# A causal decay attention with its MLP on one core: decays of k put ahead of loads in one group, the opening written out by hand, the decay of the state on ScalarE

## The chip, the core and the metric

The kernel runs on one NeuronCore of a Trainium2 chip. The metric is the device time of one execution in microseconds, the median of several executions. The engines are TensorE (PE, its weight loads are PEld), VectorE (DVE), ScalarE (ACT), GpSimd (POOL) and SyncE (SP). Each works through its own instructions in the order in which the program gives them, and they wait for each other by semaphores. Loads that turn f32 into bf16 are issued by GpSimd; stores and DMA transposes are issued by SyncE.

## What is computed

A linear attention with a decay `lam` per head, over 4 batches, 8 heads, 768 positions and head size 64, and behind it an MLP with an exact GELU (512 to 2048 to 512) on the 3072 tokens:

```python
intra = einsum(qb, kb) * Dmask            # inside a block, lam ** (i - j) for i >= j
out   = intra @ vb + (qb * lam_pow) @ kv_state
kv_state = lam_block * kv_state + (kb * rev_pow).T @ vb
...
h = x @ w_in
g = 0.5 * h * (1.0 + erf(h / sqrt(2)))
y = g @ w_out
```

The kernel takes blocks of 128 positions instead of 64, which gives the same sums.

## The kernel before

**Tiling.** There are 24 chunks of 128 positions (`NCH`), 6 for each batch (`NB`). A chunk holds all 8 heads. Four chunks (`M`) make a group of 512 tokens, and there are 6 groups (`NG`). The MLP works by groups: `mlp_blocks` (L226) gives 16 first products `mm1` (L235, four matmuls of 512 columns into `h_ps`, then GELU on ScalarE, L237) and then the second products `mm2` (L247), four to a block, with a copy by ScalarE (L252) and a store by SyncE (L253) for each 128 tokens. The attention of group g + 1 is placed between the MLP blocks of group g; the attention of group 0 stands ahead of all of it and is called the opening here.

**A chunk's steps.** `begin` takes the loaded tiles q, k and v. `decay_k` (L146) makes `k_dec`, k times a decay: eight ScalarE instructions (L153) for chunks 0 and 1, else one GpSimd instruction (L155). `transposes` (L157) turns k and q by TensorE (L161) into one PSUM bank `t_ps`, and copies them out as `kT` and as `qT` (times the decay, L168). From chunk 8 on `dma_transposes` (L170) does it instead: SyncE issues a DMA transpose of k (L174), GpSimd makes `q_hat` (L175), and SyncE issues a DMA transpose of `q_hat` (L176). `scores` (L178) makes the scores `sc_ps` (L183), the state product `kv_ps` (L190), the masked scores `sc_m` on VectorE (L195), the new state `state` (L199, L201) and its decayed copy `old` (L204) that the next chunk's state adds: VectorE makes `old` in the opening, GpSimd later. `outputs` (L207) adds the product with the state (L213) and the one with `sc_m` (L217) in `o_ps` and casts it into the group's `x_t` (ScalarE L221 in the opening, VectorE L223 later). The last chunk of a batch (5, 11, 17, 23) needs no `k_dec` and no new state.

**What sets the order.** The order is written out by hand (`manual_schedule`). In the opening a loop over s (L299 to L311) issues `transposes` and `decay_k` of chunk s, `scores` of chunk s - 1 and `outputs` of chunk s - 2. GpSimd issues the 12 loads of chunks 0 to 3 first, then the weights, then the loads of chunks 4 to 7. For the later chunks the list `todo` (L319 to L326) gives each of four steps a due point on a scale of MLP cost: kind 0 (`begin`, the DMA transposes, `decay_k`, and `prefetch`, which issues the loads of the chunks up to n + 5), kind 1 (`transposes`, group 0's MLP only), kind 2 (`scores`), kind 3 (`outputs`). `first`, `end` and `fs` set these points; a step is issued before the first MLP block that reaches its point.

**Buffers.** q, k and v have 8 buffers each, the work tiles (`kT`, `qT`, `k_dec`, `state`, `old`, `sc_m`, `q_hat`) 3 each, and PSUM has one bank each for the tags `t` and `o` and two each for `sc`, `mh` and `mo`.

Of the kernel before, what the change touches and what calls it, by code (L numbers as in the profile page):

```python
# [15 lines left out]
def kernel(  # L16
# [23 lines left out]
    M = 4  # L40
# [8 lines left out]
    work_pool = ctx.enter_context(tc.tile_pool(name="work", bufs=3))  # L49
# [21 lines left out]
    pos = consts.tile([128, 1], F32)  # L71
# [21 lines left out]
    ident = consts.tile([128, 128], BF16)  # L93
# [3 lines left out]
    warm = consts.tile([128, 1], F32)  # L97
# [8 lines left out]
    lam_q = consts.tile([128, HP, C], F32)  # L106
# [3 lines left out]
    lam_c = consts.tile([128, HP], F32)  # L110
# [12 lines left out]
    lam_c_b = lam_c[:, :, None].to_broadcast((128, HP, D))  # L123

    def make_dmask():
        nc.vector.tensor_mul(dmask, cmask[:, None, :].to_broadcast((128, H, C)),
                             lam_m[:, :, None].to_broadcast((128, H, C)))
# [5 lines left out]
    xT = {}  # L133
    states = {}

    def bank(shape, dtype, tag, name):
        return ps.tile(shape, dtype, tag=tag, name=name, bufs=2 if tag in ("sc", "mh", "mo") else 1)

    def begin(n, early=False):
        c = Chunk()  # L140
        c.n, c.sb, c.early = n, n % NB, early
        c.sc_tag = "mo" if early and n % 2 else "sc"
        c.q, c.k, c.v = (raw.pop((n, name)) for name in "qkv")
        return c

    def decay_k(c, eng):  # L146

        if c.sb == NB - 1:
            return
        c.k_dec = work_pool.tile([128, H, D], BF16, tag="kd", name="k_dec")  # L150
        if eng is nc.scalar:
            for h in range(H):
                nc.scalar.activation(c.k_dec[:, h, :], c.k[:, h, :], ACT.Copy, scale=lam_k[:, h:h + 1])  # L153
        else:
            eng.tensor_mul(c.k_dec, c.k, lam_k[:, :, None].to_broadcast((128, H, D)))  # L155

    def transposes(c):  # L157
        t_ps = bank([128, 2, HP, C], BF16, "mh" if c.early else "t", "t_ps")
        for i, src in ((0, c.k), (1, c.q)):
            for hp in range(HP):  # L160
                nc.tensor.transpose(t_ps[:, i, hp, :], src[:, 2 * hp:2 * hp + 2, :], ident)  # L161
        c.kT = work_pool.tile([128, HP, C], BF16, tag="kT", name="kT")
        c.qT = work_pool.tile([128, HP, C], BF16, tag="qT", name="qT")
        if c.early:
            nc.scalar.copy(c.kT, t_ps[:, 0])
        else:
            nc.vector.tensor_copy(c.kT, t_ps[:, 0])  # L167
        nc.vector.tensor_mul(c.qT, t_ps[:, 1], lam_q)  # L168

    def dma_transposes(c):  # L170
        c.kT = work_pool.tile([128, HP, C], BF16, tag="kT", name="kT")
        c.qT = work_pool.tile([128, HP, C], BF16, tag="qT", name="qT")
        q_hat = work_pool.tile([128, H, D], BF16, tag="qh", name="q_hat")
        nc.sync.dma_start_transpose(out=c.kT, in_=c.k.rearrange("p h d -> p (h d)"))  # L174
        nc.gpsimd.tensor_mul(q_hat, c.q, lam_p[:, :, None].to_broadcast((128, H, D)))  # L175
        nc.sync.dma_start_transpose(out=c.qT, in_=q_hat.rearrange("p h d -> p (h d)"))  # L176

    def scores(c):  # L178
        sc_ps = [bank([128, HP, C], F32, c.sc_tag, f"sc_ps{hi}") for hi in range(2)]
        for hp in range(HP):  # L180
            for hi in range(2):
                p = slice(hi * D, (hi + 1) * D)
                nc.tensor.matmul(sc_ps[hi][:, hp, :], c.kT[p, hp, :], c.qT[p, hp, :], start=True, stop=True)  # L183
        more = c.sb < NB - 1
        if more:
            kv_ps = bank([128, HP, D], F32, "t", "kv_ps")
            for hp in range(HP):
                for hi in range(2):
                    h = 2 * hp + hi
                    nc.tensor.matmul(kv_ps[hi * D:(hi + 1) * D, hp, :], c.k_dec[:, h, :], c.v[:, h, :],  # L190
                                     start=True, stop=True)
        c.sc_m = work_pool.tile([128, HP, 2, C], BF16, tag="sc_m", name="sc_m")
        dmask_r = dmask.rearrange("p (hp hi) i -> p hp hi i", hi=2)
        for hi in range(2):
            nc.vector.tensor_mul(c.sc_m[:, :, hi, :], sc_ps[hi], dmask_r[:, :, hi, :])  # L195
        if more:
            new = work_pool.tile([128, HP, D], BF16, tag="state", name="state")
            if c.sb == 0:
                nc.vector.tensor_copy(new, kv_ps)  # L199
            else:  # L200
                nc.vector.tensor_add(new, kv_ps, states[c.n][1])  # L201
            old = work_pool.tile([128, HP, D], F32, tag="old", name="old")
            if c.sb < NB - 2:
                (nc.vector if c.early else nc.gpsimd).tensor_mul(old, new, lam_c_b)  # L204
            states[c.n + 1] = new, old

    def outputs(c, x_t, off):  # L207
        o_ps = bank([128, HP, C], F32, "o", "o_ps")
        if c.sb > 0:
            for hp in range(HP):  # L210
                for hi in range(2):
                    p = slice(hi * D, (hi + 1) * D)
                    nc.tensor.matmul(o_ps[p, hp, :], states[c.n][0][p, hp, :], c.qT[p, hp, :],  # L213
                                     start=(hp == 0), stop=False, skip_group_check=True)
        for hp in range(HP):
            for hi in range(2):
                nc.tensor.matmul(o_ps[hi * D:(hi + 1) * D, hp, :], c.v[:, 2 * hp + hi, :], c.sc_m[:, hp, hi, :],  # L217
                                 start=(c.sb == 0 and hp == 0), stop=True, skip_group_check=True)
        x_o = x_t[:, :, off * C:(off + 1) * C]
        if c.early:  # L220
            nc.scalar.copy(x_o, o_ps)  # L221
        else:
            nc.vector.tensor_copy(x_o, o_ps)  # L223
# [65 lines left out]
    def prefetch(upto):  # L289
        while next_load[0] <= min(upto, NCH - 1):  # L290
            for name in "kqv":
                load(next_load[0], name)
            next_load[0] += 1
# [2 lines left out]
    alloc_x(0)  # L296
    live = {}
    make_dmask()
    for s in range(M + 2):  # L299
        if s < M:  # L300
            live[s] = begin(s, early=True)
            if s == 2:
                load_w_in(0)
            transposes(live[s])
            decay_k(live[s], nc.scalar if s < 2 else nc.gpsimd)
            if s == 1:
                nc.scalar.activation(warm, pos, ACT.Gelu)
        if 0 <= s - 1 < M:
            scores(live[s - 1])
        if s >= 2:  # L310
            outputs(live[s - 2], xT[0], s - 2)  # L311
    for s in range(1, NS):
        load_w_in(s)
    for s in range(NS):
# [5 lines left out]
    for n in range(M, NCH):  # L320
        g, i = n // M - 1, n % M
        first, end = (0.66, 1.0) if g == 0 else (0.0, 0.97)
        at = lambda f: (g + first + (end - first) * (i + f) / M) * total
        fs = (-0.5, 0.0, 0.5, 1.05) if g == 0 else (-1.0, 0.0, 0.35, 0.75)
        todo += [(at(f), kind, n) for kind, f in enumerate(fs)]
    todo.sort()  # L326

    def step(kind, n):
        g = n // M - 1
        if kind == 0:  # L330
            live[n] = begin(n)
            if g > 0:
                dma_transposes(live[n])
            decay_k(live[n], nc.gpsimd)
            prefetch(n + 5)
        elif kind == 1:
            if g == 0:
                transposes(live[n])
        elif kind == 2:
            scores(live[n])  # L340
        else:
            outputs(live[n], xT[g + 1], n % M)

# [2 lines left out]
    for g in range(NG):  # L346
        if g + 1 < NG:
            alloc_x(g + 1)
        for run, cost in mlp_blocks(g):
            while todo and todo[0][0] <= done:  # L350
                step(*todo.pop(0)[1:])
            run()
            done += cost
        for item in [t for t in todo if t[2] // M == g + 1]:
            todo.remove(item)
            step(*item[1:])
# [30 lines left out]
```

## Time and profile before

| | us |
|---|---|
| median of 3 runs (lowest, highest) | 239.39 (237.59, 240.59) |
| the profiled execution, its own time | 239.67 |
| its span, first to last instruction | 237.5 |
| TensorE matmuls busy in it | 209.7 (88%) |
| GpSimd busy in it | 111.6 (47%) |
| ScalarE busy in it | 86.0 (36%) |
| VectorE busy in it | 62.7 (26%) |

The profile is one execution of the program. Busy time says how long an engine had an instruction under way; what sets the end is read from the places where TensorE waits. The chain that ended last gives 70% of the span to TensorE, 14% to GpSimd and 11% to DMA. The timeline lists instructions in order of time, merged where like follows like; a wait stands in brackets at the end, with what ended it. The windows view gives each engine's busy time, the granted clock of TensorE (1.00 is 2.4 GHz, 0.50 is 1.2 GHz) and the DMA share in stretches of the span.

### The profile page before, as it was taken

The numbers are of one execution on the slowest core, as the hardware profiler recorded it, in microseconds if no ns is written. First come the engines' busy times: TensorE is split into PE (matmuls) and PEld (weight loads), VectorE is DVE, ScalarE is ACT, GpSimd is POOL, SyncE is SP. The second block draws the span as 40 slices with busy tenths as digits, with TensorE's granted clock in tenths as the row PEclk, the third lists the DMA queues.
The fourth block names the chain that finished last, engine by engine and source line by source line (L and its number), as shares of the span: only waits on it lengthen the run. The fifth ranks groups of instructions, "written<-read, shape, count | busy, mean of one in ns | idle before, by whom it ended". The sixth has DMA issues, their size and how long they took to land.

```text
span 237.5 us, 3783 instructions
## 1 busy us (share of the span) xinstructions
PE 209.7 (88%) x1528; PEld 102.5 (43%) x1552; DVE 62.7 (26%) x111; ACT 86.0 (36%) x158; POOL 111.6 (47%) x132
## 2 busy tenths in 40 slices
PE   1576999993198999999999999999999999999994
PEld 0355344441044444444444444444444444444453
DVE  3396000264034333132223213222321323100000
ACT  6862365000004552106650125621056510266211
POOL 8997236899717949901684696004403200000000
PEclk9999999999569999999999999999999999999998
DMA  7999999999985999994969999601433101110012
GB/s 51 146 149 199 202 207 159 153 188 138 149 35 135 114 88 95 134 171 110 92 56 101 109 168 170 63 0 47 134 89 68 22 26 65 44 44 0 32 59 88
DMA packets 100272, 24.36 MB, mean 103 GB/s; under 512 B 92960, under 2 KB 97312, under 8 KB 100256
## 3 DMA queue, kind: packets, MB, share of 16 engines
q0 software_dynamic: 79104, 13.64, 79.7%
q1 hardware_dynamic: 21152, 10.50, 20.2%
q8 instruction: 12, 0.20, 0.4%
q14 instruction: 4, 0.03, 0.1%
HBM read 27.27 MB, written 6.29 MB: 141 GB/s over the span
## 4 chain that ended last, share of the span: by engine, by line
PE 70%; POOL 14%; DMA 11%; issue 3%; DVE 0%; ACT 0%; POOLq 0%
PE o_ps L247 30%; PE h_ps L235 30%; DMA w_out_t<-in_moe_w_out_dram 8%; DMA k_t<-in_k_dram 3%; POOL v_t L65 3%; POOL q_t L65 3%; POOL k_t L65 3%; PE o_ps L217 3%; PE sc_ps L183 2%; PE o_ps L213 2%; POOL k_dec L155 2%; PE kv_ps L190 2%; PE o_ps L262 1%; POOL w_in_t L87 1%; POOL w_out_t L91 1%
## 5 line engine op out<-in xcount | busy, mean ns | idle before, releaser
L235 PE MATMUL h_ps<-x_t,w_in_t 128*128 128x512 bf16 x372 | 88.0, 386 | 2.3 <-DVE x_t L223 0.8
L247 PE MATMUL o_ps<-w_out_t,g_t 128*128 128x512 bf16 x356 | 83.7, 385 | 1.8 <-issue 1.7
L237 ACT ACTIVATE g_t<-h_ps 128x512 bf16<-128x512 f32 x96 | 57.3, 597 | 41.0 <-PE h_ps L235 41.0
L235 PEld LDWEIGHTS <-w_in_t 128*128 128x128 bf16 x384 | 36.8, 99 | 45.5 <-issue 4.6
L247 PEld LDWEIGHTS <-g_t 128*128 128x128 bf16 x368 | 34.4, 99 | 40.4 <-issue 1.7
L252 ACT COPY o_sb<-o_ps 128x512 f32<-128x512 f32 x23 | 13.5, 585 | 96.0 <-PE o_ps L247 87.8
L195 DVE TENSOR_TENSOR sc_m<-sc_ps,dmask 128x512 bf16<-128x512 f32 x48 | 30.9, 685 | 62.5 <-PE sc_ps L183 62.5
L204 POOL TENSOR_TENSOR old<-state,lam_c 128x256 f32<-128x256 bf16 x12 | 7.3, 611 | 61.4 <-DVE state L201 35.3
L65 POOL DMA_DIRECT2D q_t<-in_q_dram x24 | 21.4, 894 | 5.4 <-DMA w_out_t<-in_moe_w_out_dram 3.3
L65 POOL DMA_DIRECT2D k_t<-in_k_dram x24 | 22.0, 915 | 3.7 <-DMA w_out_t<-in_moe_w_out_dram 1.7
L65 POOL DMA_DIRECT2D v_t<-in_v_dram x24 | 21.3, 889 | 5.0 <-DMA w_in_t<-in_moe_w_in_dram 1.7
L223 DVE CAST x_t<-o_ps 128x512 bf16<-128x512 f32 x20 | 13.8, 690 | 35.6 <-PE o_ps L217 35.6
L155 POOL TENSOR_TENSOR k_dec<-k_t,lam_k 128x512 bf16<-128x512 bf16 x18 | 19.0, 1058 | 0.0
L175 POOL TENSOR_TENSOR q_hat<-q_t,lam_p 128x512 bf16<-128x512 bf16 x16 | 16.7, 1046 | 0.0
L190 PE MATMUL kv_ps<-v_t,k_dec 128*64 128x64 bf16 x160 | 6.9, 212 | 10.5 <-POOL k_dec L155 9.1
L217 PE MATMUL o_ps<-sc_m,v_t 128*64 128x128 bf16 x192 | 10.8, 240 | 0.0
L183 PE MATMUL sc_ps<-qT,kT 64*128 64x128 bf16 x192 | 10.4, 233 | 0.3 <-DVE qT L168 0.2
L190 PEld LDWEIGHTS <-k_dec 128*64 128x64 bf16 x160 | 4.8, 119 | 12.9 <-POOL k_dec L155 9.3
L161 PE MATMUL t_ps<-ident,k_t 128*128 128x128 bf16 x32 | 4.2, 275 | 6.8 <-DMA k_t<-in_k_dram 6.3
L183 PEld LDWEIGHTS <-kT 64*128 64x128 bf16 x192 | 6.0, 99 | 9.5 <-issue 8.0
L213 PE MATMUL o_ps<-qT,state 64*64 64x128 bf16 x160 | 8.9, 235 | 0.7 <-ACT x_t L221 0.7
L167 DVE COPY kT<-t_ps 128x512 bf16<-128x512 bf16 x4 | 1.7, 424 | 28.2 <-PE t_ps L161 28.1
(39 smaller groups left out, 70.6 us busy)
## 6 DMA issues: line engine op xcount, KB each, us to landing
out_dram<-o_sb SPq DMA_DIRECT2D x23, 256.0 KB, 2.2
k_t<-in_k_dram POOLq DMA_DIRECT2D x24, 128.0 KB, 4.4
q_t<-in_q_dram POOLq DMA_DIRECT2D x24, 128.0 KB, 5.5
v_t<-in_v_dram POOLq DMA_DIRECT2D x24, 128.0 KB, 6.1
w_in_t<-in_moe_w_in_dram POOLq DMA_DIRECT2D x4, 512.0 KB, 8.4
w_out_t<-in_moe_w_out_dram POOLq DMA_DIRECT2D x4, 512.0 KB, 15.4
kT<-k_t SPq DMA_TRANSPOSE x16, 4.0
qT<-q_hat SPq DMA_TRANSPOSE x16, 4.1
```

Of the source, the lines that this page charges most:

```text
L65: nc.gpsimd.dma_start(raw[n, name], chunk_of(name, n))
L155: eng.tensor_mul(c.k_dec, c.k, lam_k[:, :, None].to_broadcast((128, H, D)))
L175: nc.gpsimd.tensor_mul(q_hat, c.q, lam_p[:, :, None].to_broadcast((128, H, D)))
L183: nc.tensor.matmul(sc_ps[hi][:, hp, :], c.kT[p, hp, :], c.qT[p, hp, :], start=True, stop=True)
L190: nc.tensor.matmul(kv_ps[hi * D:(hi + 1) * D, hp, :], c.k_dec[:, h, :], c.v[:, h, :], start=True, stop=True)
L195: nc.vector.tensor_mul(c.sc_m[:, :, hi, :], sc_ps[hi], dmask_r[:, :, hi, :])
L213: nc.tensor.matmul(o_ps[p, hp, :], states[c.n][0][p, hp, :], c.qT[p, hp, :], start=(hp == 0), stop=False, skip_group_check=True)
L217: nc.tensor.matmul(o_ps[hi * D:(hi + 1) * D, hp, :], c.v[:, 2 * hp + hi, :], c.sc_m[:, hp, hi, :], start=(c.sb == 0 and hp == 0), stop=Tru ...
L223: nc.vector.tensor_copy(x_o, o_ps)
L235: nc.tensor.matmul(h_ps, w_in_t[:, ki, kf * 128:(kf + 1) * 128], x_t[:, ki, :], start=(ki == 0), stop=(ki == NK1 - 1))
L237: nc.scalar.activation(g_t[:, kf, :], h_ps, ACT.Gelu)
L247: nc.tensor.matmul(om[io], g_t[:, kf, io * C:(io + 1) * C], w_out_t[:, kf, :], start=(kf == 0), stop=(kf == NK2 - 1))
```

## The change

The opening's loop gives way to an order written out call by call, in which a chunk's scores come before the next chunk's transposes, the state product is a function of its own (`next_state`) that is called later than the scores, and outputs come earlier. In the opening k and q are transposed into two banks (tags `mh` and `mo`), `kT` of chunk 0 is copied by VectorE, the scores all use the tag `sc`, `old` is made by four ScalarE instructions of 64 columns, one for each pair of heads, and the GELU table is loaded ahead of the decays. In the list of due points chunk 8 begins at -0.45 instead of -1.0, and each begin issues the loads up to chunk n + 4 instead of n + 5.

```diff
     def transposes(c):
-        t_ps = bank([128, 2, HP, C], BF16, "mh" if c.early else "t", "t_ps")
-        for i, src in ((0, c.k), (1, c.q)):
+        if c.early:
+            t_ps = [bank([128, HP, C], BF16, tag, "t_ps") for tag in ("mh", "mo")]
+        else:
+            both = bank([128, 2, HP, C], BF16, "t", "t_ps")
+            t_ps = [both[:, 0], both[:, 1]]
+        for dst, src in zip(t_ps, (c.k, c.q)):
...
-        if c.early:
-            nc.scalar.copy(c.kT, t_ps[:, 0])
+        if c.early and c.n > 0:
+            nc.scalar.copy(c.kT, t_ps[0])
...
-        sc_ps = [bank([128, HP, C], F32, c.sc_tag, f"sc_ps{hi}") for hi in range(2)]
+        sc_ps = [bank([128, HP, C], F32, "sc", f"sc_ps{hi}") for hi in range(2)]
...
+    def next_state(c):
+        if c.sb == NB - 1:
+            return
+        kv_ps = bank([128, HP, D], F32, "t", "kv_ps")
...
-            if c.sb < NB - 2:
-                (nc.vector if c.early else nc.gpsimd).tensor_mul(old, new, lam_c_b)
+        if c.early:
+            for hp in range(HP):
+                nc.scalar.activation(old[:, hp, :], new[:, hp, :], ACT.Copy, scale=lam_c[:, hp:hp + 1])
+        elif c.sb < NB - 2:
+            nc.gpsimd.tensor_mul(old, new, lam_c_b)
...
-    for s in range(M + 2):
...
+    nc.scalar.activation(warm, pos, ACT.Gelu)
+    def early(s):
+        live[s] = begin(s, early=True)
+        transposes(live[s])
+        decay_k(live[s], nc.scalar if s < 2 else nc.gpsimd)
+    early(0)
+    scores(live[0])
+    early(1)
+    next_state(live[0])
+    outputs(live[0], xT[0], 0)
+    scores(live[1])
+    load_w_in(0)
+    early(2)
+    next_state(live[1])
+    early(3)
+    outputs(live[1], xT[0], 1)
+    scores(live[2])
+    next_state(live[2])
+    outputs(live[2], xT[0], 2)
+    scores(live[3])
+    outputs(live[3], xT[0], 3)
+    next_state(live[3])
...
-        fs = (-0.5, 0.0, 0.5, 1.05) if g == 0 else (-1.0, 0.0, 0.35, 0.75)
+        fs = (-0.5, 0.0, 0.5, 1.05) if g == 0 else (-0.45 if n == 2 * M else -1.0, 0.0, 0.35, 0.75)
...
-            prefetch(n + 5)
+            prefetch(n + 4)
...
             scores(live[n])
+            next_state(live[n])
```

On GpSimd, in the MLP of group 0, the place between the loads of chunk 10 and the state's decays, before. `k_dec_656` and `q_hat_652` are chunk 8's, `k_t_658`, `664` and `670` are the loads of chunks 11, 12 and 13, and `k_dec_681` is chunk 6's:

```order
L175 TENSOR_TENSOR q_hat_652<-q_t_538,lam_p_125 128x512
L155 TENSOR_TENSOR k_dec_656<-k_t_536,lam_k_127 128x512
L65 DMA k_t_658<-in_k_dram 128x8x64
L65 DMA q_t_660<-in_q_dram 128x8x64
L65 DMA v_t_662<-in_v_dram 128x8x64
L65 DMA k_t_664<-in_k_dram 128x8x64
L65 DMA q_t_666<-in_q_dram 128x8x64
L65 DMA v_t_668<-in_v_dram 128x8x64
L65 DMA k_t_670<-in_k_dram 128x8x64
L65 DMA q_t_672<-in_q_dram 128x8x64
L65 DMA v_t_674<-in_v_dram 128x8x64
L155 TENSOR_TENSOR k_dec_681<-k_t_406,lam_k_127 128x512
```

And now, from the loads of chunk 9 on (`k_t_586` is chunk 9's load, `667` chunk 10's, `727` chunk 11's; `k_dec_665` is chunk 6's, `k_dec_725` chunk 7's, `old_757` the decay of the state that chunk 6 made):

```order
L65 DMA k_t_586<-in_k_dram 128x8x64
L65 DMA q_t_588<-in_q_dram 128x8x64
L65 DMA v_t_590<-in_v_dram 128x8x64
L154 TENSOR_TENSOR k_dec_665<-k_t_422,lam_k_127 128x512
L65 DMA k_t_667<-in_k_dram 128x8x64
L65 DMA q_t_669<-in_q_dram 128x8x64
L65 DMA v_t_671<-in_v_dram 128x8x64
L154 TENSOR_TENSOR k_dec_725<-k_t_428,lam_k_127 128x512
L65 DMA k_t_727<-in_k_dram 128x8x64
L65 DMA q_t_729<-in_q_dram 128x8x64
L65 DMA v_t_731<-in_v_dram 128x8x64
L212 TENSOR_TENSOR old_757<-state_755,lam_c_128 128x256
```

The decay of chunk 6 moved from behind the loads of chunk 13 to right behind those of chunk 9. What follows `old_757` is chunk 8's `q_hat`, its `k_dec` and the loads of chunk 12.

On ScalarE, in the opening, before, from `kT` of chunk 1 on (`k_dec_178` is chunk 1's; the casts into `x_t_141` are those of chunks 0 to 3):

```order
L165 COPY kT_174<-t_ps_165 128x512
L153 ACTIVATE k_dec_178<-k_t_93,lam_k_127 128x64 x8
L307 ACT_TABLE_LOAD
L307 ACTIVATE warm_117<-pos_83 128x1
L165 COPY kT_224<-t_ps_215 128x512
L221 CAST x_t_141<-o_ps_256 128x4x128
L165 COPY kT_275<-t_ps_266 128x512
L221 CAST x_t_141<-o_ps_307 128x4x128
L221 CAST x_t_141<-o_ps_351 128x4x128
L221 CAST x_t_141<-o_ps_369 128x4x128
```

And now, from the same place to the last cast and the decay behind it:

```order
L169 COPY kT_190<-t_ps_180 128x512
L152 ACTIVATE k_dec_194<-k_t_93,lam_k_127 128x64 x8
L210 ACTIVATE old_214<-state_212,lam_c_128 128x64 x4
L229 CAST x_t_141<-o_ps_219 128x4x128
L169 COPY kT_253<-t_ps_243 128x512
L210 ACTIVATE old_270<-state_268,lam_c_128 128x64 x4
L169 COPY kT_285<-t_ps_275 128x512
L229 CAST x_t_141<-o_ps_291 128x4x128
L210 ACTIVATE old_333<-state_331,lam_c_128 128x64 x4
L229 CAST x_t_141<-o_ps_338 128x4x128
L229 CAST x_t_141<-o_ps_369 128x4x128
L210 ACTIVATE old_398<-state_396,lam_c_128 128x64 x4
```

Four sets of four decays of the state came in between the copies and casts; the cast of chunk 2 (`o_ps_338`) stands behind the decay of the state that chunk 2 made (`old_333`).

## Rows read from the trace of the kernel before

**Rows 1.** The page's busy tenths in 40 slices of 5.94 us, TensorE and its clock.

```profile
PE   1576999993198999999999999999999999999994
...
PEclk9999999999569999999999999999999999999998
```

**Rows 2.** Who waited for whom: total us, times, longest.

```profile
PE kv_ps L190 <- POOL k_dec L155: 9.1, 1, 9.1
```

**Rows 3.** Timeline, end of group 0: start us, us, engine, line, what, count, idle before.

```profile
42.92 1.05 POOL L155 TENSOR_TENSOR k_dec<-k_t,lam_k 128x512 bf16<-128x512 bf16 x1
...
46.84 0.32 PE L190 MATMUL kv_ps<-v_t,k_dec 128*64 128x64 bf16 x8
...
49.37 0.88 POOL L65 DMA_DIRECT2D k_t<-in_k_dram  x1
...
49.83 1.90 PE L247 MATMUL o_ps<-w_out_t,g_t 128*128 128x512 bf16 x8
49.97 1.36 SPq L174 DMA_TRANSPOSE kT<-k_t  x1
...
52.00 1.08 POOL L175 TENSOR_TENSOR q_hat<-q_t,lam_p 128x512 bf16<-128x512 bf16 x1
...
55.07 0.40 PE L183 MATMUL sc_ps<-qT,kT 64*128 64x128 bf16 x8
...
63.46 2.05 POOL L155 TENSOR_TENSOR k_dec<-k_t,lam_k 128x512 bf16<-128x512 bf16 x2
...
64.57 0.43 PE L190 MATMUL kv_ps<-v_t,k_dec 128*64 128x64 bf16 x8 [9.11 <-POOL k_dec L155]
...
64.93 3.59 PE L247 MATMUL o_ps<-w_out_t,g_t 128*128 128x512 bf16 x8
...
65.54 0.61 POOL L204 TENSOR_TENSOR old<-state,lam_c 128x256 f32<-128x256 bf16 x1
...
69.21 0.41 PE L217 MATMUL o_ps<-sc_m,v_t 128*64 128x128 bf16 x8
...
76.30 0.40 PE L183 MATMUL sc_ps<-qT,kT 64*128 64x128 bf16 x8
```

**Rows 4.** Windows: stretch, length, busy (count) of PE, PEld, DVE, ACT, POOL; clock, DMA, GB/s.

```profile
23.60:28.20 4.60, 4.38 (x11) 1.60 (x12) 0.00 (x0) 1.19 (x2) 1.40 (x2) 1.00 1.23 201
...
64.50:68.60 4.10, 4.03 (x19) 1.76 (x20) 0.42 (x1) 0.00 (x0) 1.62 (x3) 0.50 1.95 81
...
73.60:106.80 33.20, 32.77 (x244) 15.40 (x248) 8.92 (x15) 11.31 (x19) 23.12 (x26) 1.00 1.41 124
```

**Rows 5.** Timeline of the opening, to the first product of the MLP.

```profile
7.90 2.02 ACT L153 ACTIVATE k_dec<-k_t,lam_k 128x64 bf16<-128x64 bf16 x8
...
12.98 1.20 DVE L204 TENSOR_TENSOR old<-state,lam_c 128x256 f32<-128x256 bf16 x1
...
14.76 0.61 PE L161 MATMUL t_ps<-ident,q_t 128*128 128x128 bf16 x4 [0.18 <-DMA q_t<-in_q_dram]
...
15.24 1.28 DVE L195 TENSOR_TENSOR sc_m<-sc_ps,dmask 128x512 bf16<-128x512 f32 x2
...
16.43 0.41 DVE L201 TENSOR_TENSOR state<-kv_ps,old 128x256 bf16<-128x256 f32 x1
...
22.96 0.58 ACT L221 CAST x_t<-o_ps 128x512 bf16<-128x512 f32 x1 [1.29 <-PE o_ps L217]
23.60 0.59 PE L235 MATMUL h_ps<-x_t,w_in_t 128*128 128x512 bf16 x1 [0.68 <-ACT x_t L221]
```

**Rows 6.** DMA issues from 49.3 to 53.2: out, queue, count, KB, us to landing.

```profile
k_t<-in_k_dram POOLq DMA_DIRECT2D x1, 128.0 KB, 8.2
...
kT<-k_t SPq DMA_TRANSPOSE x1, 7.9
```

**Rows 7.** DMA issues from 53.9 to 56.5, same columns: the load of v for chunk 11.

```profile
v_t<-in_v_dram POOLq DMA_DIRECT2D x1, 128.0 KB, 8.1
```

**Rows 8.** The tile qT, all its DMA transposes.

```profile
DMA to landing us min/median/max: 2.4/4.1/7.3
```

More of the change, by code (lines that the diff above doesn't have):

```diff
@@ L141, in begin @@
         c.n, c.sb, c.early = n, n % NB, early
-        c.sc_tag = "mo" if early and n % 2 else "sc"
         c.q, c.k, c.v = (raw.pop((n, name)) for name in "qkv")
@@ L157, in transposes @@
     def transposes(c):
-        t_ps = bank([128, 2, HP, C], BF16, "mh" if c.early else "t", "t_ps")
-        for i, src in ((0, c.k), (1, c.q)):
+        if c.early:
[4 more added lines that the diff above has]
+        for dst, src in zip(t_ps, (c.k, c.q)):
             for hp in range(HP):
-                nc.tensor.transpose(t_ps[:, i, hp, :], src[:, 2 * hp:2 * hp + 2, :], ident)
+                nc.tensor.transpose(dst[:, hp, :], src[:, 2 * hp:2 * hp + 2, :], ident)
         c.kT = work_pool.tile([128, HP, C], BF16, tag="kT", name="kT")
         c.qT = work_pool.tile([128, HP, C], BF16, tag="qT", name="qT")
-        if c.early:
-            nc.scalar.copy(c.kT, t_ps[:, 0])
-        else:
-            nc.vector.tensor_copy(c.kT, t_ps[:, 0])
-        nc.vector.tensor_mul(c.qT, t_ps[:, 1], lam_q)
+        if c.early and c.n > 0:
+            nc.scalar.copy(c.kT, t_ps[0])
+        else:
+            nc.vector.tensor_copy(c.kT, t_ps[0])
+        nc.vector.tensor_mul(c.qT, t_ps[1], lam_q)
     def dma_transposes(c):
@@ L183, in scores @@
                 nc.tensor.matmul(sc_ps[hi][:, hp, :], c.kT[p, hp, :], c.qT[p, hp, :], start=True, stop=True)
[L184 to L191, printed above, removed]
         c.sc_m = work_pool.tile([128, HP, 2, C], BF16, tag="sc_m", name="sc_m")
@@ L195, in scores @@
             nc.vector.tensor_mul(c.sc_m[:, :, hi, :], sc_ps[hi], dmask_r[:, :, hi, :])
[L196 to L202, printed above, removed]
-            if c.sb < NB - 2:
-                (nc.vector if c.early else nc.gpsimd).tensor_mul(old, new, lam_c_b)
-            states[c.n + 1] = new, old
+    def next_state(c):
[3 more added lines that the diff above has]
+        for hp in range(HP):
+            for hi in range(2):
+                h = 2 * hp + hi
+                nc.tensor.matmul(kv_ps[hi * D:(hi + 1) * D, hp, :], c.k_dec[:, h, :], c.v[:, h, :],
+                                 start=True, stop=True)
+        new = work_pool.tile([128, HP, D], BF16, tag="state", name="state")
+        if c.sb == 0:
+            nc.vector.tensor_copy(new, kv_ps)
+        else:
+            nc.vector.tensor_add(new, kv_ps, states[c.n][1])
+        old = work_pool.tile([128, HP, D], F32, tag="old", name="old")
+        if c.early:
+            for hp in range(HP):
+                nc.scalar.activation(old[:, hp, :], new[:, hp, :], ACT.Copy, scale=lam_c[:, hp:hp + 1])
+        elif c.sb < NB - 2:
+            nc.gpsimd.tensor_mul(old, new, lam_c_b)
+        states[c.n + 1] = new, old
     def outputs(c, x_t, off):
@@ L298 @@
     make_dmask()
-    for s in range(M + 2):
[L300 to L311, printed above, removed]
+    nc.scalar.activation(warm, pos, ACT.Gelu)
[20 more added lines that the diff above has]
+    next_state(live[3])
     for s in range(1, NS):
```

## The prediction

> **What bounds the kernel now.** I read the page's slices first, then the list of waits, then the timeline around the slices that stand out, and last the windows and the DMA issues there.
>
> In the slices [rows 1] TensorE is at 9 tenths or more nearly everywhere from slice 4 on. Two places are not: the first four slices, the opening, and slices 9 and 10 (53 to 65 us), with 3 and 1 tenths, after which the clock digit is 5 and 6 for two slices. From slice 12 on only TensorE's own work is left, so what ends earlier ahead of it moves the end by as much.
>
> The list of waits names the hole: one wait of 9.1 us of the state product for `k_dec` [rows 2]. The timeline shows why [rows 3]. The scores of chunk 6 start at 55.07; the product behind them should follow after about 0.3 us, but starts at 64.57, because GpSimd makes the `k_dec` of chunks 6 and 7 only at 63.46, behind nine loads. The eight `mm2` matmuls behind it take 3.59 us, where eight took 1.90 before the wait. The windows give a granted clock of 0.50, the 1.2 GHz level, from 64.50 to 68.60 [rows 4]; TensorE had been idle for 9 us before.
>
> The opening ends when ScalarE casts the last chunk's output (22.96 to 23.54) and `mm1` starts at 23.60 [rows 5]. The last load that its transposes wait for, q of chunk 3, lands at 14.7. From there 8.9 us go through TensorE, VectorE and ScalarE in turn. TensorE's matmuls go at half pace here too: 11 of `mm1` take 4.38 us in 23.60 to 28.20, though the row gives the clock as 1.00 [rows 4].
>
> **The decays of k ahead of the loads.** In the new order GpSimd has the decay of chunk 6 right behind the loads of chunk 9, where k of chunk 10 stood before, at 49.37 [rows 3]. One decay takes 1.03 us (2.05 for two), so it is done at 50.4, some 4 us before its product wants it. The three loads of chunk 10 (0.88 each) end at 53.0, the decay of chunk 7 at 54.1, the loads of chunk 11 at 56.7. Chunk 7's product is wanted about 4 us after chunk 6's, at 58 or later, so it does not become the next wait.
>
> So TensorE goes from the scores of chunk 6 straight into the product. Chunk 4 shows that step: done at full pace, the product starts some 0.3 us after its scores, here at 55.4 instead of 64.57, which is 9.2 us. The stretch behind it, from 64.57 to 69.21, runs at half pace and no longer would: the eight `mm2` give back 3.59 - 1.90 = 1.7, the product 0.43 - 0.32 = 0.1, the eight transposes about 0.3 by the same ratio. Together 2.1. I bound that by 1.7 and half of 4.64, 2.3. Sum of this part: **11.3 us**.
>
> **What is late next.** Chunk 8's `qT` is made by a DMA transpose of `q_hat`, and chunk 8 now begins later. Before, GpSimd made `q_hat` at 52.00. Now it stands behind the loads of chunk 11 and behind `old` of chunk 6: 56.7 + 0.61 + 1.08 = 58.4, and then SyncE issues the transpose [rows 3]. Behind it wait the transposes of the next chunks and two stores on SyncE, none wanted sooner. How long it takes to land is bounded by 2.4 us, the least of any `qT` [rows 8], and by the 7.9 of chunk 8's `kT` [rows 6]: 60.8 to 66.3. The row that is nearest: that `kT` was issued at 49.97 and landed at 57.9, and the k that GpSimd had issued at 49.37 landed 8.2 later, at 57.6 [rows 3, 6]. So a transpose lands right behind the load issued just before it. Here that is v of chunk 11, which is issued at about the same time in both kernels and landed at 55.8 + 8.1 = 63.9 [rows 7]. I take 63.9. The scores of chunk 8 were at 76.30 [rows 3]; 11.3 less is 65.0, and by what the opening gives less still. So `qT` comes just in time, and what the opening gives beyond 1.1 us is lost again here.
>
> The Trainium skill, "DMA: Bandwidth & Descriptors", section on queues, rings and completion order, says that each DMA engine goes round-robin between the queue rows that have work. By that rule the lone transpose would not stand behind the loads, would land at about twice its least, 63.2, and the sum would be 0.1 better; the row of the `kT` that landed behind its neighbour in 7.9 us does not look like that.
>
> **The opening.** It still waits for q of chunk 3: loads and their order on GpSimd are as before, the first weight load among them. I follow the new order from there, with the opening's durations [rows 5]. The transposes of q run from 14.76 to 15.4. Then come on TensorE the two halves of chunk 1's outputs (0.6 each, as any eight of these matmuls): 16.6; scores of chunk 2: 17.2; masked scores on VectorE, 1.28: 18.5; the state, 0.41: 18.9. Now ScalarE makes `old` in four pieces. Eight pieces of 64 columns took 2.02, so four take 1.0: 19.9. Only then comes the cast of chunk 2, 0.58: 20.5. It frees the one bank `o`, so that both halves of chunk 3's outputs start: 21.7 (its masked scores are ready at 20.9 or so). Last cast: 22.3, and `mm1` at 22.4 instead of 23.60. Gain: **1.2 us**. The state product of chunk 3 lies beside that cast, the last `old` beside `mm1`.
>
> It could be nothing, since `old` on ScalarE stands in front of a cast that TensorE waits for, or 1 us worse if the pieces take twice that. Were only chunk 3's own chain left (transposes 0.6, `qT` 0.64 as half of the masked scores, scores 0.6, 1.28, outputs 0.6, cast 0.58: 4.3 behind 14.76), it would be 4.5 us. I stay with 1.2, the chain with measured pieces. The long `old` on VectorE, 1.20 us at 12.98 where GpSimd's decays begin, goes away, but nothing at that time ends the opening.
>
> The Trainium skill, "ScalarE: Activation LUTs", rules for kernel authors, budgets about 0.3 us and 0.83 ns per element for one ACTIVATE, so four pieces of 64 would be 1.4 us, an estimate from that page, and `mm1` would start 0.4 later; the 2.02 us for eight pieces say 1.0.
>
> **Edits at nothing.** The two banks for k and q and the scores on one tag change which tile a step waits for, and are in the chain above. The GELU table load and `kT` of chunk 0 on VectorE lie ahead of the wait for q of chunk 3; without that cover they would cost the 1.3 us of a load. The earlier start of the MLP does not run into chunk 4's decay: it ends at 44.0, and its product, at 46.84 before, would come at 45.6 [rows 3]. One chunk less of loads ahead is hidden by the distance of four chunks, over 30 us, between issue and use.
>
> **Sum.** 9.2 + 2.1 + 1.2 - 0.1 (the scores of chunk 8 at 63.9 instead of 63.8) = 12.4. The profiled execution took 239.67 us, so 227.3; the median, 239.39, is 0.3 less, which I leave in the range.
>
> **The rivals.**
> A. The opening gives nothing, because ScalarE is the longer way there. For it: `old` and the casts share one engine now. Against it: all pieces are measured and the chain is short. Then the scores of chunk 8 come at 65.0 with no wait: 239.67 - 11.3 = 228.4.
> B. `qT` of chunk 8 takes the place of the wait. If it lands as late as that `kT` did, 7.9 us after its issue, at 66.3, the scores of chunk 8 move by 9.95 instead of 12.4: 229.7. With about 1 us more at chunk 9, whose transpose is issued behind chunk 12's loads, 231. For it: the DMA engines are full here and one less transpose ahead is the only relief. Against it: fewer loads are outstanding when it is issued.
> C. `qT` lands early, 61 to 62, and the opening gives 2 to 3 us: 225.3. For it: the transposes that landed in 2.4. Against it: loads are under way all the time.
> D. Slower. GpSimd becomes the bound in the middle groups, since its loads are issued a chunk later, behind its waits for the states, and a chunk's GpSimd work no longer fits TensorE's time for a chunk. In group 1 TensorE has 33.2 us for four chunks, 8.3 each, and GpSimd is busy for 23.1, 5.8 each [rows 4]. It begins to decide when 2.5 us are added to a chunk. At 3.5 us more, 16 chunks lose 1.0 each, 16 us, more than the 12.4: 243. Against it: nothing in the change adds to GpSimd's work there.
>
> **How the numbers follow.** Forecast 0.60, A 0.16, B 0.16, C 0.06, D 0.02. The range takes in B with its second wait, and C: 224.8 to 231.0. About 2% is what a measurement of this kernel can tell from no change; only D, and a B twice as long, lie outside the faster side: faster 0.96, same 0.03, slower 0.01.
>
> **What would show it.** In the new profile: no wait of the state product for `k_dec` in group 0, no slices at 1 or 3 tenths behind the opening, and no granted clock of 0.50 there; the first `mm1` at 22 to 23; the scores of chunk 8 near 64, and if TensorE waits ahead of them, for a transpose of `q_hat`, by under 2 us; from there to the end as long as before (161 us). I would be wrong if another wait of several us stood between 45 and 75 us, if the clock fell again, or if the groups behind chunk 8 took longer.

## The result and the profile after

| | before | after |
|---|---|---|
| median, us (lowest to highest, executions) | 239.99 (237.59 to 241.51, 4) | 226.90 (226.38 to 227.22, 4) |
| ratio to before, 95% interval | | 0.948 (0.941 to 0.956) |
| profiled execution, us | 239.67 | 226.88 |
| first `mm1` | 23.60 | 22.82 |
| scores of chunk 6 | 55.07 | 53.14 |
| scores of chunk 8 | 76.30 | 63.57 |
| from there to the end of the span | 161.2 | 161.2 |

The forecast was 227.3. The ratio is one of means and leaves out the slowest of the four runs before (241.51), which counts as a slow run, so it is not 226.90 / 239.99. The slices of the changed kernel, 5.62 us each, show TensorE and its granted clock:

```profile
PE   0668999989899999999999999999999999999993
...
PEclk9999999999999999999999999999999999999999
```

The slices at 3 and 1 tenths behind the opening [rows 1] are gone, and so are the clock digits 5 and 6. The timeline of the place where the wait was, with columns as in [rows 3]:

```profile
43.85 1.05 POOL L154 TENSOR_TENSOR k_dec<-k_t,lam_k 128x512 bf16<-128x512 bf16 x1
...
44.96 0.32 PE L200 MATMUL kv_ps<-v_t,k_dec 128*64 128x64 bf16 x8
...
50.15 1.09 POOL L154 TENSOR_TENSOR k_dec<-k_t,lam_k 128x512 bf16<-128x512 bf16 x1
...
53.14 0.40 PE L187 MATMUL sc_ps<-qT,kT 64*128 64x128 bf16 x8
53.47 0.32 PE L200 MATMUL kv_ps<-v_t,k_dec 128*64 128x64 bf16 x8
...
53.72 1.90 PE L255 MATMUL o_ps<-w_out_t,g_t 128*128 128x512 bf16 x8
...
58.09 1.05 POOL L179 TENSOR_TENSOR q_hat<-q_t,lam_p 128x512 bf16<-128x512 bf16 x1
...
59.17 1.19 SPq L180 DMA_TRANSPOSE qT<-q_hat  x1
...
63.57 0.40 PE L187 MATMUL sc_ps<-qT,kT 64*128 64x128 bf16 x8 [0.43 <-DMA qT<-q_hat]
```

The decay of chunk 6 stands at 50.15, 3 us ahead of the scores, and the state product follows them after 0.33 us, without a wait. The eight `mm2` behind it take 1.90 us again, not 3.59 [rows 3]. One small wait is new: the scores of chunk 8 wait 0.43 us for the DMA transpose of `q_hat`. The opening of the changed kernel, answering to [rows 5]:

```profile
15.39 0.60 PE L165 MATMUL t_ps<-ident,q_t 128*128 128x128 bf16 x4 [0.23 <-DMA q_t<-in_q_dram]
...
22.82 0.59 PE L243 MATMUL h_ps<-x_t,w_in_t 128*128 128x512 bf16 x1 [0.46 <-ACT x_t L229]
...
23.62 5.60 PE L243 MATMUL h_ps<-x_t,w_in_t 128*128 128x512 bf16 x22 [0.22 <-issue]
```

q of chunk 3 is transposed 0.63 later than before, yet `mm1` starts 0.78 earlier: 7.43 us lie between the two instead of 8.84. The last row holds 22 matmuls in 5.60 us, 0.25 each; before, 11 took 4.38, 0.40 each [rows 4]. TensorE reached its full pace sooner in this execution.

So the 12.73 us by which the scores of chunk 8 moved are three pieces: 0.78 at the first `mm1`; 1.15 from there to the scores of chunk 6 (31.47 to 30.32); and 10.80 from the scores of chunk 6 to those of chunk 8 (21.23 to 10.43).

### The profile page after: what moved, and what is told of

Same layout as the page of the kernel before. It is cut to its first block, busy times and chain, and to the rows that moved or that the text cites. A ratio compares the mean times of both kernels' runs of the same rounds, so it can differ in the third digit from the quotient of the medians.

```text
span 224.8 us, 3796 instructions
## 1 busy us (share of the span) xinstructions
PE 206.5 (92%) x1528; PEld 101.4 (45%) x1552; DVE 61.0 (27%) x108; ACT 89.1 (40%) x173; POOL 111.6 (50%) x132
## 4 chain that ended last, share of the span: by engine, by line
PE 69%; POOL 14%; DMA 12%; issue 3%; ACT 0%; POOLq 0%
PE h_ps L243 30%; PE o_ps L255 29%; DMA w_out_t<-in_moe_w_out_dram 8%; POOL q_t L65 4%; POOL v_t L65 3%; POOL k_t L65 3%; PE o_ps L225 2%; PE sc_ps L187 2%; DMA k_t<-in_k_dram 2%; PE o_ps L221 2%; DMA qT<-q_hat 2%; PE o_ps L270 2%; POOL k_dec L154 1%; PE kv_ps L200 1%; POOL w_in_t L87 1%
## 5 line engine op out<-in xcount | busy, mean ns | idle before, releaser
L243 PE MATMUL h_ps<-x_t,w_in_t 128*128 128x512 bf16 x372 | 86.9, 382 | 2.0 <-DVE x_t L231 0.8
L255 PE MATMUL o_ps<-w_out_t,g_t 128*128 128x512 bf16 x356 | 82.0, 379 | 1.8 <-issue 1.7
L212 POOL TENSOR_TENSOR old<-state,lam_c 128x256 f32<-128x256 bf16 x12 | 7.4, 616 | 49.4 <-DVE state L206 25.9
L221 PEld LDWEIGHTS <-state 64*64 64x64 bf16 x160 | 5.5, 113 | 7.7 <-issue 7.5
L225 PEld LDWEIGHTS <-v_t 128*64 128x64 bf16 x192 | 6.7, 117 | 3.4 <-issue 1.8
```

What stands on the lines that cost most here:

```text
L243: nc.tensor.matmul(h_ps, w_in_t[:, ki, kf * 128:(kf + 1) * 128], x_t[:, ki, :], start=(ki == 0), stop=(ki == NK1 - 1))
L255: nc.tensor.matmul(om[io], g_t[:, kf, io * C:(io + 1) * C], w_out_t[:, kf, :], start=(kf == 0), stop=(kf == NK2 - 1))
```

## The experiments

The theory was that the decays put ahead of the loads give 11.3 us, which needs both edits to the list of due points, and that the opening gives about 1 us on top, through its order. The rivals were that one edit does it all, that the transpose of `q_hat` takes the gain back, and later that something in the opening other than its order carries it. Each median is over 4 to 10 executions. The kernels ran in four sets, each on its own chip and apart from the changed kernel: the first four, then `old` on VectorE with the three moves of loads, then the banks, then the last two. One kernel that ran in two of these sets gave medians 0.66 us apart, so across sets a difference of that size tells nothing by itself, and the rows have to carry it.

**The decays alone.** The kernel before with the two numbers changed.

```diff
-fs = ... else (-1.0, 0.0, 0.35, 0.75)
+fs = ... else (-0.45 if n == 2 * M else -1.0, 0.0, 0.35, 0.75)
-            prefetch(n + 5)
+            prefetch(n + 4)
```

> The kernel before with only the two edits of the order of GpSimd (chunk 8 begins at -0.45, loads four chunks ahead); the opening is the old one. My theory: the whole wait of the state product for k_dec goes and nothing takes its place, since without the gain of the opening the scores of chunk 8 come at 65.0, behind a qT that lands at 63 to 64: 239.7 - 11.3 = 228.4 us, no wait for qT, first product of the MLP at 23.6 as before and its half pace to 28 us as before. Rival 1, the opening and the decays are worth their sum: 226.9 + 1.9 = 228.8. Rival 2, the old opening delays the decays too and part of the wait stays: over 231.

Measured 227.96 (227.44 to 228.68), ratio 0.950 (0.945 to 0.955). The timeline of its opening and of its scores:

```profile
11.26 2.01 ACT L153 ACTIVATE k_dec<-k_t,lam_k 128x64 bf16<-128x64 bf16 x8
...
13.29 1.28 ACT L307 ACT_TABLE_LOAD   x1
...
14.70 0.57 ACT L165 COPY kT<-t_ps 128x512 bf16<-128x512 bf16 x1
...
15.25 0.61 PE L161 MATMUL t_ps<-ident,q_t 128*128 128x128 bf16 x4
15.30 0.69 DVE L168 TENSOR_TENSOR qT<-t_ps,lam_q 128x512 bf16<-128x512 bf16 x1 [1.11 <-ACT kT L165]
...
24.27 5.06 PE L235 MATMUL h_ps<-x_t,w_in_t 128*128 128x512 bf16 x15 [0.68 <-ACT x_t L221]
...
55.20 0.40 PE L183 MATMUL sc_ps<-qT,kT 64*128 64x128 bf16 x8
...
65.13 0.40 PE L183 MATMUL sc_ps<-qT,kT 64*128 64x128 bf16 x8
```

From the scores of chunk 6 to those of chunk 8 it takes 9.93 us against 21.23, so 11.3 less, with no wait for the transpose. `mm1` starts at 24.27 and not at 23.6 as expected, since q of chunk 3 is 0.49 later here. The sum of the parts (228.8) was the rival; the measured 227.96 is under both numbers and doesn't tell them apart. What is left for the opening is 227.96 - 226.90 = 1.06 us, by two medians of different sets.

**The opening alone.** The changed kernel with both numbers put back.

> The changed kernel with the old order of GpSimd (chunk 8 begins at -1.0, loads five chunks ahead), so only the opening is new. My theory: the time is unchanged, 239 to 240 us, although the first product of the MLP starts 0.8 to 1.2 us earlier, because k_dec of chunk 6 is made at about 63.5 by GpSimd, whose times hang on loads, and TensorE waits for it there, now 10 to 11 us instead of 9.1. Rival, gains add up: 237.7 us with the wait at 9.1.

Measured 239.67 (239.19 to 241.15), ratio 1.000 (0.997 to 1.003). The wait stands in its list of waits, and in its timeline:

```profile
PE kv_ps L200 <- POOL k_dec L154: 10.8, 1, 10.8
```

```profile
63.33 2.05 POOL L154 TENSOR_TENSOR k_dec<-k_t,lam_k 128x512 bf16<-128x512 bf16 x2
...
64.44 0.42 PE L200 MATMUL kv_ps<-v_t,k_dec 128*64 128x64 bf16 x8 [10.81 <-POOL k_dec L154]
```

`mm1` starts at 22.54 here, 1.06 earlier than before, but GpSimd makes the decays at 63.33, at 63.46 before [rows 3]. What the opening gives is waited off again: the wait is 10.8 instead of 9.1.

**One of the two numbers.** The changed kernel with the loads five chunks ahead again, and the changed kernel with chunk 8 begun at -1.0 again.

> The changed kernel with loads five chunks ahead again; chunk 8 still begins at -0.45. My theory, by GpSimd's order: k_dec of chunk 6 stands behind the loads of chunk 10 and is done at 53.9, so its product waits some 0.4 us; the loads of chunk 12 stand ahead of q_hat of chunk 8, which is issued as a transpose at 62 instead of 59.2 and lands at 66 to 67, so that the scores of chunk 8 wait 3 us: 230 us, between 229 and 233. Rival, the begin point alone does it and the number of loads ahead is worth nothing: 227.

> The changed kernel with chunk 8 beginning at -1.0 again; loads stay four chunks ahead. My theory: q_hat and k_dec of chunk 8 and the nine loads of chunks 10 to 12 stand ahead of the decay of chunk 6, which ends at 61 to 62, so the state product waits 8 to 9 us and the clock falls: 237 us, between 236 and 239. Rival, one chunk less of loads ahead brings the decay early enough and most of the gain stays: under 232.

Measured 229.75 (228.37 to 231.10) and 236.77 (235.77 to 237.82). The first keeps most of the gain. Its list of waits:

```profile
PE h_ps L243 <- DVE x_t L231: 1.8, 1, 1.8
PE sc_ps L187 <- DMA qT<-q_hat: 1.3, 2, 1.1
```

The wait for `qT` grew from 0.4 to 1.3, the product of chunk 6 waits 0.3 us for `k_dec` (expected: 0.4), and `mm1` of group 1 waits 1.8 us (0.8 in the changed kernel) for an `x_t` that is late because `old` of chunk 6 stands behind the loads of chunk 12. The cause was as expected, but not the sizes: I had put 3 us on `qT` and nothing on that `x_t`. The second has the long wait still:

```profile
PE kv_ps L200 <- POOL k_dec L154: 8.8, 1, 8.8
```

There GpSimd has three loads fewer ahead of the decays and makes them at 60.30 instead of 63.33, which is the 3 us. So the later begin of chunk 8 gives 9.9 (239.67 to 229.75), and the shorter lead of the loads 2.9, with or without the other.

**The decay of the state on VectorE.** The opening as changed, with `old` made there as before.

```diff
-            for hp in range(HP):
-                nc.scalar.activation(old[:, hp, :], new[:, hp, :], ACT.Copy, scale=lam_c[:, hp:hp + 1])
+            nc.vector.tensor_mul(old, new, lam_c_b)
```

> The changed kernel with the decay of the state in the opening on VectorE again (one instruction instead of four on ScalarE). My theory: no change, within 0.3 us of 226.9: the cast of chunk 2 comes some 0.7 us earlier, but the last outputs wait for the masked scores of chunk 3, which VectorE ends at the same time or up to 0.4 later, and the scores of chunk 8 wait for qT anyway. Rival, the placement on ScalarE is what shortens the opening: 228 us, as with the old opening.

Measured 226.91 (226.06 to 227.84), ratio 0.946 (0.941 to 0.950): the engine of that decay doesn't matter. The rows say the same. From the transposes of q of chunk 3, at 15.14, to `mm1`, at 22.55, it takes 7.41, against 7.43. The cast of chunk 2 does come sooner, 4.28 behind those transposes instead of 4.93, but the last outputs wait for the masked scores of chunk 3, as expected:

```profile
21.30 0.59 PE L224 MATMUL o_ps<-sc_m,v_t 128*64 128x128 bf16 x7 [0.33 <-DVE sc_m L191]
```

**The banks or the order.** First the changed kernel with k and q transposed into one bank; then the decays alone with the two banks and the scores on one tag, in the old order of the opening. Both ran on one chip in turn.

```diff
-            t_ps = [bank([128, HP, C], BF16, tag, "t_ps") for tag in ("mh", "mo")]
+            both = bank([128, 2, HP, C], BF16, "mh", "t_ps")
+            t_ps = [both[:, 0], both[:, 1]]
```

> The changed kernel, with k and q of a chunk in the opening transposed into one bank again, as before. The opening's own worth was 1.06 us (227.96 with the decays alone, 226.90 with both). Theory, the order: what was gained lies in the written-out order, since the chain behind q of chunk 3 has one last chunk in it and its kT is copied long before its q lands; 226.9, within 0.4, and the first mm1 7.5 us behind the landing of q of chunk 3. Rival, the banks: VectorE's qT waits for ScalarE's kT in the same bank, and most of the gain goes; 228.0, and mm1 8.5 to 9 us behind that landing.

> The kernel before with the decays of k ahead of the loads, and in the opening the two banks for k and q and the scores on one tag, in the old order of steps, with old on VectorE and the state product among the scores. Theory, the order: the banks alone give nothing; 228.0, within 0.4, as the decays alone did (227.96), mm1 about 9 us behind the landing of q of chunk 3. Rival, the banks: 227.0, mm1 about 7.5 us behind that landing.

Measured 227.53 (227.22 to 227.74), ratio 0.946 (0.943 to 0.949), and 226.25 (225.31 to 227.21), ratio 0.941 (0.937 to 0.946). The theory of the order falls: the old order with two banks is the faster of the two, and at the rival's 227.0 or under it; the kernel with one bank in the written-out order lies between theory and rival, 0.6 above the changed kernel. That 0.6 is between two sets, and the ratios to the kernel before, 0.946 and 0.948, don't show it; so what counts is that these two kernels are 1.3 apart in one set, and the rows. The waits of VectorE in the opening with one bank, and its timeline:

```profile
DVE qT L173 <- ACT kT L170: 3.8, 3, 1.6
```

```profile
15.44 0.61 PE L166 MATMUL t_ps<-ident,q_t 128*128 128x128 bf16 x4 [0.23 <-DMA q_t<-in_q_dram]
...
17.34 0.56 ACT L170 COPY kT<-t_ps 128x512 bf16<-128x512 bf16 x1
...
17.93 0.69 DVE L173 TENSOR_TENSOR qT<-t_ps,lam_q 128x512 bf16<-128x512 bf16 x1 [1.60 <-ACT kT L170]
...
23.64 5.58 PE L244 MATMUL h_ps<-x_t,w_in_t 128*128 128x512 bf16 x20 [0.46 <-ACT x_t L230]
```

And the timeline of the two banks in the old order:

```profile
12.73 0.68 DVE L172 TENSOR_TENSOR qT<-t_ps,lam_q 128x512 bf16<-128x512 bf16 x1
...
13.08 0.57 ACT L169 COPY kT<-t_ps 128x512 bf16<-128x512 bf16 x1
...
14.90 0.60 PE L165 MATMUL t_ps<-ident,q_t 128*128 128x128 bf16 x4 [0.25 <-DMA q_t<-in_q_dram]
...
15.54 0.69 DVE L172 TENSOR_TENSOR qT<-t_ps,lam_q 128x512 bf16<-128x512 bf16 x1
...
22.13 7.17 PE L239 MATMUL h_ps<-x_t,w_in_t 128*128 128x512 bf16 x27 [0.68 <-ACT x_t L225]
```

With one bank, VectorE's `qT` waits until ScalarE has copied `kT` out of the same bank, and ScalarE's copy stands behind other work: in the decays alone, behind `k_dec` and the table load, until 15.30 for chunk 2. With two banks that `qT` runs at 12.73, ahead of `kT`. From the transposes of q of chunk 3 to `mm1`, by these rows:

| | old order | written-out order |
|---|---|---|
| one bank | 8.84 (before), 9.02 (decays alone) | 8.20 |
| two banks | 7.23 | 7.43 (after) |

The banks carry the gain, 1.6 to 1.8 in the old order and 0.8 in the new; the order gives 0.6 to 0.8 with one bank and nothing with two. In the old order the scores went onto one tag together with the two banks, so the two were not told apart. Each length is of one profile, but it repeats: seven further profiles of kernels with two banks in the written-out order have 7.41 to 7.43, and the eighth ran at another pace (last section).

**The loads.** Three moves in the changed kernel. The first puts q and k ahead of v in the opening and the loads of chunk 7 behind the decay of chunk 4; the second issues the loads of chunk 11 one chunk later, behind chunk 8's `q_hat`, so that its transpose stands ahead of them; the third kernel has both.

```diff
-    for n in range(M):
-        for name in "kqv":
-            load(n, name)
+    for item in "k0 q0 k1 q1 v0 k2 q2 v1 k3 q3 v2 v3".split():
+        load(int(item[1]), item[0])
...
-            prefetch(n + 4)
+            prefetch(n + (3 if n == 2 * M - 1 else 4))
...
-    prefetch(2 * M - 1)
+    prefetch(2 * M - 2)
```

> The changed kernel with the first twelve loads in another order (v of a chunk behind k and q of the next) and the loads of chunk 7 behind the decay of chunk 4. My theory: q of chunk 3 lands one load, 0.9 us, earlier and the first product of the MLP starts at about 21.9 instead of 22.8, but the time stays at 226.9 (226.5 to 227.2), because the transpose of chunk 8's q_hat is issued at the same time and the scores of chunk 8 wait for it, now 1.3 us instead of 0.4. Rival, the opening's gain passes through: 226.0.

> The changed kernel with the loads of chunk 11 behind chunk 8's q_hat and k_dec instead of ahead of them. My theory: q_hat is made 2 us earlier, qT of chunk 8 lands near 61.5, the wait of 0.4 us goes and nothing takes its place: 226.5 us. Rival, the transpose lands no earlier, since DMA engines are full: 226.9.

> Both of the former two together. My theory: the scores of chunk 8 no longer wait, so the earlier opening passes through: 225.5 us, 1.0 less than with the loads of chunk 11 later alone and 1.4 less than the changed kernel. Rival, another wait (chunk 4's decay, chunk 9's transpose) takes it back: 226.5.

Measured 226.04 (225.54 to 226.63), 226.93 (225.84 to 227.33) and 225.23 (224.13 to 225.99). In the first my theory fell and the rival's 226.0 came: I had thought that an earlier `mm1` would be waited off at `qT` of chunk 8. Its timeline:

```profile
14.34 0.61 PE L164 MATMUL t_ps<-ident,q_t 128*128 128x128 bf16 x4 [0.25 <-DMA q_t<-in_q_dram]
...
21.77 2.72 PE L242 MATMUL h_ps<-x_t,w_in_t 128*128 128x512 bf16 x6 [0.46 <-ACT x_t L228]
...
47.89 1.12 POOL L153 TENSOR_TENSOR k_dec<-k_t,lam_k 128x512 bf16<-128x512 bf16 x1
...
56.90 1.30 SPq L179 DMA_TRANSPOSE qT<-q_hat  x1
...
62.54 0.40 PE L186 MATMUL sc_ps<-qT,kT 64*128 64x128 bf16 x8
```

`mm1` comes 1.05 earlier, as q does, and GpSimd's decay of chunk 6 2.3 earlier, for which I have a likely reason but no experiment: GpSimd no longer waits for k of chunk 3 in the opening, so the weights behind it go out sooner. So the transpose is issued 2.3 earlier too, and nothing waits. In the second chunk 8's `qT` lands at 61.5, as expected, and its wait is gone, but it only went to the next chunk; that the rival's 226.9 came has this other reason. Its waits and its timeline:

```profile
PE sc_ps L187 <- DMA qT<-q_hat: 0.6, 1, 0.6
```

```profile
65.08 1.20 SPq L180 DMA_TRANSPOSE qT<-q_hat  x1
...
72.38 0.40 PE L187 MATMUL sc_ps<-qT,kT 64*128 64x128 bf16 x8 [0.64 <-DMA qT<-q_hat]
```

Chunk 9's transpose now finds five loads under way instead of three, and takes 7.2 us instead of 4.8. The third kernel came out near the 225.5 expected.

**The order once more, without the wait for `qT`.** The three moves of the loads in the written-out order and in the old order with two banks, on one chip in turn.

> The kernel with the opening's loads reordered, chunk 7's loads behind chunk 4's decay and chunk 11's loads a chunk later, once more, beside the next kernel: 225.2, as before, first mm1 near 21.8.

> The same three moves of loads, in the kernel with the two banks and the old order of the opening: against the kernel before it in this call only the written-out order, the state product apart from the scores and the decay of the state on ScalarE are undone. Theory, the banks: with them the written-out order gives nothing; within 0.4 of 225.2, first mm1 7.3 to 7.5 us behind the landing of q of chunk 3. Rival, the order costs: 224.6, since the old order took 226.25 where the written-out one took 226.90. Second rival, the order gives: 226 or more.

Measured 225.89 (224.41 to 226.74), ratio 0.942 (0.937 to 0.947), and 226.08 (225.57 to 226.83), ratio 0.944 (0.939 to 0.948). The first is the same kernel that took 225.23 before, so 0.66 us lies between two medians of one kernel, and the two readings have to be set against each other and not against 225.2: they are 0.2 apart, with ranges that overlap. The order gives nothing that these runs can tell, neither rival is borne out (the 226.08 has the second's number, but not the distance that it stood for), and the second kernel's chain has the length of the table, 7.51:

```profile
14.14 0.61 PE L164 MATMUL t_ps<-ident,q_t 128*128 128x128 bf16 x4 [0.31 <-DMA q_t<-in_q_dram]
...
21.65 0.59 PE L238 MATMUL h_ps<-x_t,w_in_t 128*128 128x512 bf16 x1 [0.68 <-ACT x_t L224]
```

For the same reason as the 0.66 the worth of the moved loads, about 1 us against the changed kernel, is at the edge of what these runs tell; that this kernel beats the changed one rests on two medians out of two, and on the kernel with `old` on VectorE, whose 226.91 stands in one set with the 225.23.

## Why the forecast held, and which reason did not

**The wait and what follows from it (9.2 and 2.1).** The state product came 0.33 behind its scores instead of 9.50, which is 9.17. From the scores of chunk 6 to those of chunk 8 the rest is 10.80 - 9.17 = 1.63, and 2.06 with the wait of 0.43 taken off. Both terms were right, and the decays alone measured their sum, 11.3, by themselves.

**What is late next (0.1).** The mechanism was right: the transpose comes just in time. It was issued at 59.17, not 58.4, because GpSimd was 0.8 later from the decay of chunk 6 on (50.15, forecast 49.4). It landed about 63.4, forecast 63.9, and TensorE came at 63.14, forecast 63.8. The term measured 0.43. Of the landing, the place was right and the sizes were not. The chain of waits has the transpose, and the list of issues v of chunk 11, which is issued at 56.62:

```profile
59.17 4.26 DMA qT<-q_hat
```

```profile
v_t<-in_v_dram POOLq DMA_DIRECT2D x1, 128.0 KB, 5.5
```

I had taken 8.1 us for that v and nothing from there to the transpose. It took 5.5, so it landed at 62.1, and the transpose 1.3 behind it: two errors that nearly cancel, which is luck. That a transpose has its place among the loads holds beyond this one: of the 24 in the changed kernel that have a load issued behind them, 22 landed after the load issued just before and ahead of the one issued just after. By the rule of the Trainium skill, "DMA: Bandwidth & Descriptors", queues, rings and completion order, a lone transpose shares the engines by turns and would take near twice its least, 4.8, an estimate. The 4.26 alone can't tell; the 7.2 us with five loads under way in the kernel with chunk 11's loads later don't fit that, and fit a place behind the loads.

**The opening (1.2).** The chain gave 1.41, since 8.84 became 7.43, but q of chunk 3 was 0.63 later, so `mm1` gained 0.78. The 0.63 is not shown to come from the change: with the same order of these loads, the profiles have that start anywhere from 14.76 to 15.44. So the size was near, but the reason was wrong. I followed the new order and said that the two banks "change which tile a step waits for, and are in the chain above", as an edit at nothing. They were in it, because the chain let `qT` of chunk 3 start without ScalarE's `kT`; but then the gain is theirs. Had I read the waits of VectorE in the opening, I would have found `qT` waiting for `kT` there, 4.1 us in three times:

```profile
DVE qT L168 <- ACT kT L165: 4.1, 3, 2.0
```

```profile
14.63 0.69 DVE L168 TENSOR_TENSOR qT<-t_ps,lam_q 128x512 bf16<-128x512 bf16 x1 [0.45 <-ACT kT L165]
...
17.23 0.68 DVE L168 TENSOR_TENSOR qT<-t_ps,lam_q 128x512 bf16<-128x512 bf16 x1
```

The last of the three is chunk 2's, at 14.63. What VectorE has behind it then holds up chunk 3's `qT` until 17.23, 2.47 behind the transposes of its q; with two banks in the old order it is 0.64 (15.54 behind 14.90). The way through `old` on ScalarE and the cast of chunk 2, by which I had sized the 1.2, is no bound by itself: with `old` on VectorE that cast comes sooner and the chain is as long. The Trainium skill has the rule, "PSUM — Partial Sum Buffer", section on bank collisions: the compiler's scheduler puts a dependency between any two instructions of different engines that touch one bank in the same 32 partitions, two reads as well. The traces agree: 3.8 us of such waits with one bank, none with two.

**The clock in the opening (not in the sum).** TensorE went at half pace from the first `mm1` until 28.2 before and until 24.9 after. That is the 1.15 us from `mm1` to the scores of chunk 6, which I hadn't forecast. It made good what the late q (0.63) and the wait for `qT` (0.43) took. Without it TensorE would have come to the scores of chunk 8 1.15 us later and not have waited there, so the time would have been some 0.7 us longer, an estimate. That it came is luck, as far as these runs tell: from `mm1` to the scores of chunk 6 the profiles of this case take 30.0 to 31.6 us, and the kernel with `old` on VectorE, with the same chain ahead of it, took 31.59 (22.55 to 54.14), at half pace until 27.2. So the change is not shown to bring the clock up sooner, and what does stays open.

**Edits at nothing.** `old` on ScalarE was right: VectorE does as well. Its four pieces took 1.05 to 1.07 us, as the eight of [rows 5] said, not the 1.4 estimated from the Trainium skill, "ScalarE: Activation LUTs", rules for kernel authors. The decay of chunk 4 was closer than I said: I gave its product 1.6 us behind it, and the rows above show it done at 44.90 and the product at 44.96. One us more from the opening and TensorE would have waited there, had GpSimd stayed. The `kT` on VectorE, the scores on one tag and the table load were not tried by themselves.

**The rivals.** A, B and C are out by the rows: the opening's chain is 1.41 shorter, the transpose costs 0.43, and it landed at 63.4. D is out, since the stretch behind chunk 8 is as long as before, 161.2.

## What to carry to other kernels

Where one engine waits for several us in one place, look at what stands ahead of the late instruction in its releaser's queue, and move that, then ask which instruction was moved behind it: here `q_hat`, by 0.43. An opening's gain is worth nothing until the wait behind it is gone (239.67 with the opening alone), so parts must be added in the order in which waits end. Two engines that read out of one PSUM bank waited for each other here: look at a short chain's waits for the other engine's copy before its order. And a time that comes out as forecast proves the total, not the terms: here a late q and a wait of 0.43 stood against an earlier clock, and nearly cancelled.

## What the runs showed of the hardware

**One kernel's opening goes at either pace of TensorE.** The profiled execution of the first of the last two kernels took 224.41, the least of its six; the same kernel's other profile took 225.57, with 0.61 us for the four transposes and 7.43 to `mm1`. Its timeline and windows (columns as in [rows 3] and [rows 4]):

```profile
14.05 0.40 PE L164 MATMUL t_ps<-ident,q_t 128*128 128x128 bf16 x4 [0.55 <-DMA q_t<-in_q_dram]
...
20.21 0.59 PE L242 MATMUL h_ps<-x_t,w_in_t 128*128 128x512 bf16 x1 [0.46 <-ACT x_t L228]
```

```profile
16.00:18.00 2.00, 1.10 (x24) 0.84 (x24) 1.53 (x4) 1.25 (x5) 2.00 (x4) 1.00 1.25 203
18.00:20.00 2.00, 1.02 (x24) 0.89 (x24) 1.02 (x3) 1.10 (x3) 2.00 (x4) 0.83 1.21 198
20.00:22.00 2.00, 1.57 (x4) 0.69 (x5) 0.27 (x1) 1.23 (x5) 0.94 (x2) 0.50 1.23 205
```

Four transposes take 0.40 instead of 0.61, so TensorE ran at full pace here (those of chunks 0 to 2 still took 0.61 to 0.63), and the chain to `mm1` is 6.16 us instead of 7.4; TensorE was half idle in 16 to 20, and the clock fell to 0.50 about 19.3, ahead of `mm1`. In every other profile of this case the four took 0.60 or 0.61, half pace, while the row gave the clock as 1.00 [rows 4]: the spacing of the matmuls tells the pace there, and the clock column does not. Executions of one kernel are spread over 2 us, and this is one place where they differ; what decides the pace stays open.

**GpSimd's times hang on landings long before.** In the kernel with the opening's loads reordered the weights behind the decay of chunk 3 go out 0.9 us sooner than in the changed kernel (14.72 against 15.65), and GpSimd's decay of chunk 6 comes 2.3 us sooner, over 30 us later. In between, its loads wait for weights to land (1.64 us at 38.89 in the changed kernel). The loads of chunk 7 were moved as well, so the 2.3 is not shown to come from the opening alone.
